# A hand-written order of 887 steps is replaced by another one (attention and a squared-ReLU layer on one core)

## The chip, the cores and the metric

The kernel runs on one core of one Trainium2 chip. The metric is the device time of one execution in microseconds (us), the median of several runs. A core has TensorE (PE; its weight loads are shown apart as PEld), VectorE (DVE), ScalarE (ACT), GpSimd (POOL) and SyncE (SP). Each works through its own instructions in the order in which the program issues them, and waits at an instruction until what it needs is there. SP, POOL and here and there ACT also issue DMAs.

## The reference

Attention over a sliding window of 128 keys plus 4 sink keys, and then a layer with a squared ReLU:

```python
batch, n_heads, seq, head_dim = (4, 8, 768, 64)
scores = scale * np.matmul(q, k.transpose(0, 1, 3, 2))
keep = is_sink | in_window            # 4 sinks, or 0 <= row - column < 128
a = softmax(np.where(keep, scores, -1e9))
x = np.matmul(a, v)  -> (3072, 512)   # heads side by side
h = x @ w_in                          # 512 -> 2048
g = np.maximum(h, 0.0) ** 2
out = g @ w_out                       # 2048 -> 512, float32
```

## The kernel before, in words

The kernel first builds a list of 887 **steps** (class `Op`), each one a small function that issues the instructions of one piece of work, and then issues them in the order of the string `ORDER`. A word of it is a step's number; a letter behind it picks the engine (d VectorE, a ScalarE, g POOL) where a step can run on several, and `+0` or `+1` the pool of PSUM banks where there is a choice. Nothing else sets the order. `Plan.run` goes through the words:

```python
for word in words:
    word, *chosen = word.split("+")
    n = int(word.rstrip("pdag"))
    o = self.ops[n]
    ...
    for s in o.takes:
        if len(s.pools) > 1:
            s.pool = s.pools[int(chosen.pop(0))]
        s.room = free[s.pool].pop(0)
    self.idle = DUMMIES.get(n, 0)
    o.run(o.engine)
    for s in o.reads:
        s.readers -= 1
        if not s.readers:
            free[s.pool].append(s.room)
```

A step that takes a room (a PSUM bank or an SBUF buffer) gets the one that came free first in the order of the list, and its first instruction waits for that room's last readers. There are two pools of two banks in PSUM (`att` and `den`), and rings such as `expm` (8), `r` (3), `osb` (2) in SBUF.

The work is staged by batch (0 to 3), and a batch by three pairs of 128-row tiles (s = 0, 1, 2). In each batch:

- **Loads and turns.** POOL issues loads of q, k and v, 128 KB each, that also convert to bf16 (`load_cast`, `load_v`, `load_natural`, lines L367, L376, L396, L408). In batches 0 and 1 TensorE transposes q and k (L500) and an `unload` copies them out of PSUM; in batches 2 and 3 SP issues transposing DMAs instead (`turn`, L454).
- **Attention.** `scores` (L607; 64-row matmuls, two heads side by side), `sink_scores` (L566) with `sink_keys` (L542) that lays out the sink keys, `expo` (ScalarE, L628), `domask` (VectorE, L637 or L640, or two selects on POOL, L215), `values` (L676), `norm` (VectorE: a reciprocal L692 and a product L693). The result goes back to columns by `bridge` on TensorE (L725) and `bridge_copy`, or, in batches 2 and 3, by a transposing DMA (`turn_x`, L707).
- **Layer 1.** In batches 0 and 1 plain products (L757), a `relu` (L768 on ScalarE, L770 on VectorE) and a `square` (L777, L779). In batches 2 and 3 a Strassen scheme of seven products on blocks half as large (`quad`): sums `xs` of x blocks (L845), once `spread` that separates even and odd rows, sums `wi` of weight blocks (L803, L811), products numbered 1, 2, 5, 4, 3, 6, 7 (L887), a copy `first` of product 1 (t), subtractions from t (L928), a `relu` of the first two quarters (L943), a square (L909 on ScalarE, L911 on VectorE) and a `final` sum with relu (L955).
- **Layer 2.** Plain (L976) for two pairs of batch 0, otherwise again seven products (`layer2_fast`, L1086) with sums of g blocks on VectorE (L1044), copies out of PSUM (L189 on ScalarE and L191 on VectorE, a helper's lines), pair sums (L1111, L1127, L1134) and a store (L1163; L999 in the plain form).

The steps that the prediction speaks of by number: batch 3, pairs 0 and 1: scores 654 and 638 with exps 655, 657 and 639, 641, values 636, sink scores 629. Batch 2, layer 1, pair 0, second quad: products 513 (5), 515 (4), 516 (3), 519 and 520 (6 and 7), relu 517; first quad: products 533 and 534 (6 and 7), final 535, squares 536 and 532, and 518 for the second quad. Batch 2, layer 1, pairs 1 and 2: sum 537, products 569, 570, 573, 575 (1, 2, 5, 4) with copy 571, and 583, 584, 587 (1, 2, 5) with copy 585. Around 105 us: weight sums 361 to 364, layer-2 product 451 and its copy 453, copy 456, sum 468, sink_keys 628 of batch 3, pair sum 457, product 459 (batch 1, pair 0); mask 426. Turn 615 (keys of batch 3, tile 0), turn_x 413, norm 405. Also bridge 123, scores 212 and 663, product 833 with final 827, norms 421 and 428 with scores 431, spread 504; SP's turn 383 and stores 299, 288, 318; POOL's masks 232, 234, 260 and loads 370 to 382 (batch 2) and 610 (batch 3); scores 415.

Of the kernel before, what the change touches and what calls it, by code (L numbers as in the profile page):

```python
# [25 lines left out]
170a 159 160d 177 128 131 165 173d 161d 132d 178d 166d 164a 130a 129a 133a 144 146 136 138 174 145 137 289 290 148  # L26
134 175a 140 135 176a 147d 167d 139d 291 179d 292 293 141d 142 143 149g 42 43 44 45 46 150 151 47 48 49 50 51 52 53
54 365 366 367 368 208g 369 370 371 372 373 294 295 152 154 296 153d 155d 297d 298d 186 187d 180 181a 200+0 204+1
192+0 201 193 205 194a 206d 195a 189 207d 182d 203a 196+0 197 183 198a 190a 191a 188d 199d 202d 274 212+0+0 184d 209
278 279 215 213 237+0+0 210+1 211 238 240 185d 300 301 275 214 302 241d 276 277 303 280 281 282 304 219+0+0 283 222  # L30
220 306a 305 307 230+0+0 309a 233 231 308 311 223 216 221 310 239d 224+0 312 234g 232g 299 385 386 384 383 313 225
314 242+0 217+0 243 218 284 315 316 235+0 236 285 251+0 286a 287a 317d 252d 253d 244+0 246 226+1 228 247d 227d 245a
248+1 229a 399 322 249d 250d 402 400 323d 355 401 256+0+0 259 257 340 254+0 255 341a 258d 358 356 342a 396 260d 334
335a 374 375 376 377 378 379 380 381 395g 388 390 387 288 392 391 318 389 393 394 331 263+0+0 332a 261+1 264 266 319
262 267d 324d 406 333a 407 320a 337 409 265g 382 597 268+0 598 599 600 601 602 603 604 605 606 607 608 609 610 338a
321d 403 269 328 627d 410 270+0 272 404 408 329a 271a 273d 359 325 405 339a 336a 326a 346 347d 357 327a 415 418 419d
330d 352 411 353a 416 412 354d 447 448 343 344a 345a 349 422 423 425 417g 426g 611 451 452 397 363 449 453d 350d 398
450 351a 348a 454 455 457 466 456a 438 458 459 441 439 467 485 486 489 490 487 460 488 461 361 492 431 491a 432 434
615 413 616 622 620 619 493 462 494d 468 463 464a 414 465 621 617 618 420 440g 612 424g 427 496 433g 442g 428 498
421 470 471 443 435g 436 472a 504a 495 362 499 497 500 473 444 437 508 505 469 628 501 475d 474 477 647 429 625 445  # L40
430 446 650 502a 648 624 503 623 626 360 476 478 481 507 479 506 480 364 482 483d 523+0 525a 524 631 527 526 528 634
632 509+0 510 529 511d 512 530 531a 654 538 633 539 513 514 515 655 533 534 657 649g 656g 516 517a 638 613 614 535
635 536d 537 641 519 520 532a 636 658g 651g 521 639 569+0 570 637 571a 629 583+0 630 572 573 585a 640 522a 518a 574
584 587 575 576 586 555+1 642 589 577a 588 643 679 557a 540 556 590 559 591a 592a 578a 558 560 579 580 593 594 581
561 562 595 541+0 542 683 563a 564a 543d 545 544 680 546 565 547 566 548 684 686 644 567 685a 596a 549a 582a 681
550d 689 682 645 484 646 670 551 552 687 690 673 671 674g 553 688a 554a 663 691 694 666 664 665g 568d 698 692 693
699 659 652 702 703 705 667g 672g 695 696d 700 653 717 660 718 721 668 697 661 736a 704a 669 737 675 676 701 722 739
740 738 708 677 678 662 755+1 706 709 741+1 742 757a 719 720 756 743a 723a 707d 759 745 724 758 761 725 744 760 762
763a 764a 711 746 727 710 713 726a 765 766 747 712 769 714 771 767 728 730 715d 772 748 749a 729 815+0 816 817a 732
770 731 818 733 819 751 752 787+1 734a 735 716 801+0 802 803a 789a 753 820 804 768d 821 788 822 773+1 805 791 754a  # L50
823a 824a 775a 790 806 750d 792 829 807 774 793 776 825 808 794 826 809a 827 830 831 795a 796a 810a 777 779 811 778
812 797 798 833 780 834 836 813 799 828a 835a 781a 832 838d 839 783 784 782a 800a 814a 837 840 841 844 785 786d 842
848 849 852 853 855 843 845 846d 867 854a 850 851 858 857d 868 871 847 856 859 873a 861 862 860 863 864 869 872 865a
866 870 877 874 876a 875 878 880 881 886 879 882 883 885 884
"""
DUMMIES = {
    57: 26, 63: 18, 64: 3, 83: 3, 91: 3, 97: 5, 101: 3, 119: 2,
# [1227 lines left out]
```

## Time and profile before

| | |
|---|---|
| median of 3 runs | 213.01 us (212.85 to 213.62) |
| span of the profiled execution, first to last instruction | 210.2 us (210.17) |
| instructions | 5719 |
| TensorE busy | 201.4 us, 96% of the span |
| VectorE, ScalarE, POOL busy | 170.8, 126.6, 101.8 us |
| granted TensorE clock, mean | 0.997 |
| DMA | 26.09 MB, of it 12.59 MB in POOL's converting loads |

The profiled execution's own time is known as its span; the runs' times also hold what lies around it, 2.8 us at the median. Times in microseconds that stand alone (as in "at 131.6") count from the start of the span.

How to read it: the page gives each engine's busy time and, in 40 slices of the span, its busy share in tenths. The chain follows the last instruction back, at each step to what released it. The waits view lists who waited for whom: total, times and the longest. The timeline has one row for neighbouring instructions of a kind: start, duration, engine, line, what it writes from what, and in brackets the idle time before it with what ended it. An engine that is idle but not on the chain costs nothing.

### The profile page before, as it was taken

The page shows a single profiled execution, that of the slowest core. Times are in us where ns is not written, and L with a number is a line of the kernel's source. Part 1 is how long each engine was busy: PE and PEld are TensorE (multiplying, and loading weights), DVE is VectorE, ACT ScalarE, POOL GpSimd, SP SyncE. Part 2 cuts the span into 40 slices and gives each one's busy share as a digit, 9 for nine tenths or more (in the row PEclk, how much of TensorE's full clock was granted, in tenths as well). Part 3 has the DMA queues.
Part 4 walks back from the last instruction along what each step waited for, and adds up shares of the span by engine and source line. Part 5 has one row for each costly group of instructions (what it writes and reads, how often), then busy time and mean ns, then how long its engine had stood idle before and what let it go on. Part 6 is the DMA issues. An engine that isn't in the chain of part 4 may idle for free.

```text
span 210.2 us, 5719 instructions
## 1 busy us (share of the span) xinstructions
PE 201.4 (96%) x2383; PEld 169.4 (81%) x2383; DVE 170.8 (81%) x317; ACT 126.6 (60%) x162; POOL 101.8 (48%) x143
## 2 busy tenths in 40 slices
PE   3999999999999999999999999799999999999993
PEld 3859996689468845679789988699899999999892
DVE  7487567366999964789997988999989978999863
ACT  2498287407744579898952268889870244896110
POOL 7999774898877941999369023700253000000000
PEclk9999999999999999999999999999999999999998
DMA  5999999999999999999987639700512300400222
GB/s 171 278 188 206 171 201 214 161 155 205 153 112 157 104 150 252 138 124 144 149 102 151 103 77 179 50 3 0 150 62 69 75 5 38 166 0 0 103 100 100
DMA packets 93881, 26.09 MB, mean 124 GB/s; under 512 B 86816, under 2 KB 91552, under 8 KB 93856
## 3 DMA queue, kind: packets, MB, share of 16 engines
q0 software_dynamic: 69248, 12.59, 81.3%
q1 hardware_dynamic: 24424, 13.07, 27.9%
q8 instruction: 18, 0.29, 0.6%
q10 hardware_dynamic: 184, 0.07, 0.1%
q14 instruction: 7, 0.06, 0.1%
HBM read 27.30 MB, written 6.29 MB: 160 GB/s over the span
## 4 chain that ended last, share of the span: by engine, by line
PE 94%; DVE 2%; ACT 1%; POOL 1%; issue 1%; POOLq 0%; DVEq 0%
PE py L1086 29%; PE pm L757 20%; PE pm L887 17%; PE po L676 7%; PE py L976 7%; PE ps L607 6%; PE pt L500 3%; PE pt L182 2%; PE px L725 1%; ACT expm L628 1%; PE ya L1086 1%; PE ps L600 1%; PE pk L566 1%; DVE r L955 1%; DVE gT_sb L911 0%
## 5 line engine op out<-in xcount | busy, mean ns | idle before, releaser
L215 POOL TENSOR_SCALAR_AFFINE_SELECT expm<-expm 128x512 bf16<-128x512 bf16 x42 | 29.2, 724 | 49.5 <-ACT expm L628 24.5
L628 ACT ACTIVATE expm<-ps 128x1024 bf16<-128x1024 f32 (+1 forms) x48 | 43.8, 950 | 12.4 <-PE ps L607 11.3
L757 PE MATMUL pm<-xT,w_in_sb 128*128 128x256 bf16 (+1 forms) x320 | 44.7, 294 | 0.0
L757 PEld LDWEIGHTS <-w_in_sb 128*128 128x128 bf16 x320 | 34.2, 114 | 6.6 <-issue 0.9
L1086 PEld LDWEIGHTS <-gT_sb 128*128 128x128 bf16 x336 | 31.1, 98 | 4.2 <-issue 0.5
L1086 PEld LDWEIGHTS <-sg 128*128 128x128 bf16 x240 | 22.8, 98 | 3.3 <-issue 0.5
L768 ACT ACTIVATE r<-pm 128x1024 bf16<-128x1024 f32 x14 | 14.3, 1022 | 13.5 <-PE pm L757 13.4
L887 PEld LDWEIGHTS <-w_in_sb 128*128 128x128 bf16 x256 | 21.8, 114 | 0.5 <-issue 0.2
L887 PE MATMUL pm<-xs,wi 128*128 128x128 bf16 (+1 forms) x192 | 19.5, 246 | 1.5 <-DVE xs L845 0.9
L1086 PE MATMUL py<-wt,gT_sb 128*128 128x256 bf16 x160 | 20.8, 273 | 0.0
L1086 PE MATMUL py<-wt,sg 128*128 128x256 bf16 x160 | 20.6, 273 | 0.0
L909 ACT ACTIVATE gT_sb<-r 128x1024 bf16<-128x1024 bf16 x18 | 18.4, 1051 | 0.3
L1086 PE MATMUL py<-w_out_sb,gT_sb 128*128 128x256 bf16 x144 | 18.5, 273 | 0.0
L189 ACT ACTIVATE osb<-py 128x256 f32<-128x256 f32 (+1 forms) x15 | 6.2, 410 | 20.3 <-DMA out_dram<-osb 6.0
L770 DVE TENSOR_SCALAR r<-pm 128x1024 bf16<-128x1024 f32 x10 | 12.2, 1222 | 7.5 <-PE pm L757 4.3
L887 PEld LDWEIGHTS <-wi 128*128 128x128 bf16 x192 | 16.4, 113 | 2.2 <-issue 2.1
L693 DVE TENSOR_TENSOR xn_sb<-po,rc 128x512 bf16<-128x512 f32 (+1 forms) x28 | 17.2, 615 | 1.0
L676 PEld LDWEIGHTS <-expm 128*128 128x128 bf16 x352 | 16.3, 97 | 1.4 <-issue 0.5
L676 PE MATMUL po<-v,expm 128*128 128x65 bf16 x352 | 17.3, 193 | 0.1
L943 ACT ACTIVATE r<-pm 128x1024 bf16<-128x1024 f32 x12 | 12.1, 1021 | 8.1 <-PE pm L887 7.9
L928 DVE TENSOR_TENSOR t<-t,pm 128x512 f32<-128x512 f32 x24 | 15.9, 680 | 0.9 <-ACT t L189 0.4
L955 DVE CUSTOM_DVE_ANT_1 r<-pm,t 128x1024 bf16<-128x1024 f32 x12 | 14.5, 1220 | 1.6 <-PE pm L887 1.5
(97 smaller groups left out, 381.9 us busy)
## 6 DMA issues: line engine op xcount, KB each, us to landing
out_dram<-osb SPq DMA_DIRECT2D x11, 512.0 KB, 4.5
v<-in_v_dram POOLq DMA_DIRECT2D x24, 128.0 KB, 7.1
qn<-in_k_dram POOLq DMA_DIRECT2D x20, 128.0 KB, 7.1
qn<-in_q_dram POOLq DMA_DIRECT2D x20, 128.0 KB, 6.9
w_in_sb<-in_moe_w_in_dram POOLq DMA_DIRECT2D x4, 512.0 KB, 10.2
w_out_sb<-in_moe_w_out_dram POOLq DMA_DIRECT2D x4, 512.0 KB, 10.4
qr<-in_k_dram SPq DMA_DIRECT2D x4, 256.0 KB, 5.1
qr<-in_q_dram SPq DMA_DIRECT2D x4, 256.0 KB, 4.8
```

The costliest lines, as they stand in the source:

```text
L215: nc.gpsimd.affine_select(out=e_tile, in_=e_tile, compare_op=ALU.is_ge, fill=fill, base=i - 1, pattern=[[0, n], [1 if i else -1, 128]], ch ...
L628: nc.scalar.activation(out=x[:, :, o:512], in_=bank_t["s", b, s, m][:, :, o:512], func=AF.Exp, scale=scale)
L676: touch(("po", b, s, m0), e, nc.tensor.matmul(pv[:, i, h2, :], lhsT=lhsT, rhs=rhs, start=(n_ == 0), stop=(n_ == len(mms) - 1)), j)
L693: touch(("po", b, s, m0), e, nc.vector.tensor_tensor(out=xn_sb[:, 2 * s:2 * s + 2, 128 * (m0 + j0):128 * (m0 + j0 + nj)].rearrange("p i (j ...
L757: nc.tensor.matmul(pm[:, i, :], lhsT=w_in_sb[:, fb // 4, kb, fb % 4:512:4], rhs=xT[:, c0 // 256:(c0 + cw) // 256, kb, :], start=(kb == 0), ...
L768: nc.scalar.activation(out=o, in_=h, func=AF.Relu)
L887: touch(tag, e, nc.tensor.matmul(y[:, bk, i, :], lhsT=weights(name, f0 + i, a), rhs=rhs[:, a, :], start=fresh and i == 0 and a == 0, stop= ...
L909: nc.scalar.activation(out=d, in_=x, func=AF.Square)
L928: touch(tag, e, nc.vector.tensor_tensor(out=T["t"], in0=T["t"], in1=T["y"][:, bk], op=ALU.subtract), bk)
L955: touch(tag, e, nc.vector._custom_dve(TENSOR_ADD_SAT, out=r.rearrange("p b n c -> p b (n c)"), in0=T["y"].rearrange("p b n c -> p b (n c)" ...
L976: touch((b, u), e, nc.tensor.matmul(pm[:, i, :], lhsT=gT_sb[:, fb, 128 * t:128 * t + 128], rhs=w_out_sb[:, fb, :], start=(fb == 0), stop=( ...
L1086: ins = nc.tensor.matmul(y_, lhsT=x[:, i, :], rhs=r_, start=(first or tail and n == 2) and i == 0, stop=i == HB - 1, skip_group_check=not ...
```

## The change

Only the string `ORDER` is replaced. The same 887 steps are issued, with the same matmuls and the same DMAs. The first 25 of TensorE's 290 steps and its last 5 keep their places; between them most steps move by one to twelve places. SP's 60 steps and POOL's (102, now 100) are reordered as well.

61 steps change the engine: 6 relus from VectorE to ScalarE and 4 the other way; 6 squares of plain layer 1 each way; 5 squares of the quads from VectorE to ScalarE and 1 back; 6 copies from ScalarE to VectorE and 2 back in layer 2, with 5 `first_quarter` copies and 1 `evac` from VectorE to ScalarE; 3 unloads and 4 bridge copies from ScalarE to VectorE, 3 bridge copies back; the spread 504 from ScalarE to VectorE; 5 masks from POOL to VectorE and 2 back; sink_values 627 from VectorE to POOL. Three PSUM choices change: 210 and 226 from pool 1 to 0, 244 from 0 to 1.

The places of the two strings that the prediction works on (whole lines of the diff):

```diff
...
-95+0 4 96 117 97 106g 99+1 98 104+0 107 100d 101 118g 81+1 102d 113+0 108d 156 115 127 27 28 29 30 31 32 33 34 35 36
-37 38 116d 82 109+0 111 39 40 41 119+1 121 157a 158a 110 112 120 122 162 123+1 125 163d 168 169d 126a 124a 171 172a
+95+0 4 96 117 97 106g 99+1 98 104+0 107 100d 101 118g 81+1 102d 113+0 108d 156 115 127 116d 82 109+0 119+1 121 120 122
+27 28 29 30 31 32 33 34 35 36 110 157a 111 112 158a 37 38 39 40 41 42 43 44 45 46 47 48 49 50 51 52 53 54 365 162
...
-54 365 366 367 368 208g 369 370 371 372 373 294 295 152 154 296 153d 155d 297d 298d 186 187d 180 181a 200+0 204+1
-220 306a 305 307 230+0+0 309a 233 231 308 311 223 216 221 310 239d 224+0 312 234g 232g 299 385 386 384 383 313 225
-335a 374 375 376 377 378 379 380 381 395g 388 390 387 288 392 391 318 389 393 394 331 263+0+0 332a 261+1 264 266 319
+191d 237+0+0 240 241d 238 300 301 302 239d 281 282 283 219+0+0 304 305 222 220 230+0+0 231 307 233 309a 395g 366 367
+368 369 208g 232g 234g 370 371 372 373 374 375 376 377 378 379 380 381 382 383 221 303 306d 310 223 308 311 224+0 313
+225 210+0 312 211 242+0 314 396 243 284 217+0 218 315 316 299 384 386 385 235+0 236 285 251+0 252d 253d 286a 317a 287a
+357 401 356 258d 340 254+0 332a 255 341a 333d 324d 260g 334 335a 390 389 388 393 387 394 391 392 288 318 263+0+0 264
...
-450 351a 348a 454 455 457 466 456a 438 458 459 441 439 467 485 486 489 490 487 460 488 461 361 492 431 491a 432 434
-615 413 616 622 620 619 493 462 494d 468 463 464a 414 465 621 617 618 420 440g 612 424g 427 496 433g 442g 428 498
+467 447 449 353a 354a 350a 422 346 423 351a 347a 425 343 344a 348a 345a 450 424d 448 363 364 451 453d 452 454 455 438
+361 362 456d 468 607 608 609 610 426g 439 440g 611 413 615 441 442g 612 613 628 457 485 486 458 459 397 462 398 489
...
-632 509+0 510 529 511d 512 530 531a 654 538 633 539 513 514 515 655 533 534 657 649g 656g 516 517a 638 613 614 535
-635 536d 537 641 519 520 532a 636 658g 651g 521 639 569+0 570 637 571a 629 583+0 630 572 573 585a 640 522a 518a 574
+529 530 510 513 635 512 514 633 537 654 531a 533 534 535 536d 538 539 515 516 655 657 614 649g 651g 656g 638 517a 641
+518a 569+0 519 520 636 571a 570 573 642 521 639 572 637 574 640 532a 583+0 584 629 585a 575 587 576 630 522a 586 588
...
```

A word's place in the string sets its place on its own engine's queue; between engines the waits decide.

More of the change, by code (lines that the diff above doesn't have):

```diff
@@ L23 @@
 68d 69+1 85 70 71d 103+0 84+0 105 73g 74d 72d 23 75+1 86 76 77d 91+0 78a 24 87+1 93 25 89 88 92+0 80 26 114+1 90 94
-95+0 4 96 117 97 106g 99+1 98 104+0 107 100d 101 118g 81+1 102d 113+0 108d 156 115 127 27 28 29 30 31 32 33 34 35 36
-37 38 116d 82 109+0 111 39 40 41 119+1 121 157a 158a 110 112 120 122 162 123+1 125 163d 168 169d 126a 124a 171 172a
-170a 159 160d 177 128 131 165 173d 161d 132d 178d 166d 164a 130a 129a 133a 144 146 136 138 174 145 137 289 290 148
-134 175a 140 135 176a 147d 167d 139d 291 179d 292 293 141d 142 143 149g 42 43 44 45 46 150 151 47 48 49 50 51 52 53
@@ L28 @@
-54 365 366 367 368 208g 369 370 371 372 373 294 295 152 154 296 153d 155d 297d 298d 186 187d 180 181a 200+0 204+1
-192+0 201 193 205 194a 206d 195a 189 207d 182d 203a 196+0 197 183 198a 190a 191a 188d 199d 202d 274 212+0+0 184d 209
-278 279 215 213 237+0+0 210+1 211 238 240 185d 300 301 275 214 302 241d 276 277 303 280 281 282 304 219+0+0 283 222
-220 306a 305 307 230+0+0 309a 233 231 308 311 223 216 221 310 239d 224+0 312 234g 232g 299 385 386 384 383 313 225
-314 242+0 217+0 243 218 284 315 316 235+0 236 285 251+0 286a 287a 317d 252d 253d 244+0 246 226+1 228 247d 227d 245a
@@ L33 @@
-248+1 229a 399 322 249d 250d 402 400 323d 355 401 256+0+0 259 257 340 254+0 255 341a 258d 358 356 342a 396 260d 334
-335a 374 375 376 377 378 379 380 381 395g 388 390 387 288 392 391 318 389 393 394 331 263+0+0 332a 261+1 264 266 319
-262 267d 324d 406 333a 407 320a 337 409 265g 382 597 268+0 598 599 600 601 602 603 604 605 606 607 608 609 610 338a
-321d 403 269 328 627d 410 270+0 272 404 408 329a 271a 273d 359 325 405 339a 336a 326a 346 347d 357 327a 415 418 419d
-330d 352 411 353a 416 412 354d 447 448 343 344a 345a 349 422 423 425 417g 426g 611 451 452 397 363 449 453d 350d 398
@@ L38 @@
-450 351a 348a 454 455 457 466 456a 438 458 459 441 439 467 485 486 489 490 487 460 488 461 361 492 431 491a 432 434
-615 413 616 622 620 619 493 462 494d 468 463 464a 414 465 621 617 618 420 440g 612 424g 427 496 433g 442g 428 498
-421 470 471 443 435g 436 472a 504a 495 362 499 497 500 473 444 437 508 505 469 628 501 475d 474 477 647 429 625 445
-430 446 650 502a 648 624 503 623 626 360 476 478 481 507 479 506 480 364 482 483d 523+0 525a 524 631 527 526 528 634
-632 509+0 510 529 511d 512 530 531a 654 538 633 539 513 514 515 655 533 534 657 649g 656g 516 517a 638 613 614 535
@@ L43 @@
-635 536d 537 641 519 520 532a 636 658g 651g 521 639 569+0 570 637 571a 629 583+0 630 572 573 585a 640 522a 518a 574
[L44 to L52, printed above, removed]
@@ L53 @@
-848 849 852 853 855 843 845 846d 867 854a 850 851 858 857d 868 871 847 856 859 873a 861 862 860 863 864 869 872 865a
-866 870 877 874 876a 875 878 880 881 886 879 882 883 885 884
+95+0 4 96 117 97 106g 99+1 98 104+0 107 100d 101 118g 81+1 102d 113+0 108d 156 115 127 116d 82 109+0 119+1 121 120 122
+27 28 29 30 31 32 33 34 35 36 110 157a 111 112 158a 37 38 39 40 41 42 43 44 45 46 47 48 49 50 51 52 53 54 365 162
+123+1 125 168 163d 164a 169a 124d 126d 171 172d 173a 170a 159 160d 165 161d 166d 167d 177 128 131 130a 178a 179a 174
@@ new lines @@
+129d 132d 133d 175d 145 148 149d 176d 137 140 289 290 144 146 141d 147d 136 291 134 135 138 292 150 139d 151 293 142
+143 294 295 152 154 296 274 155d 153a 275 297d 298a 186 187d 183 196+0 276 277 184a 180 185a 181a 278 200+0 201 279
+204+1 205 198a 203a 188d 202d 192+0 182d 206d 194d 193 197 207d 199d 280 195a 212+0+0 213 215 189 216 209 214 190a
+191d 237+0+0 240 241d 238 300 301 302 239d 281 282 283 219+0+0 304 305 222 220 230+0+0 231 307 233 309a 395g 366 367
+368 369 208g 232g 234g 370 371 372 373 374 375 376 377 378 379 380 381 382 383 221 303 306d 310 223 308 311 224+0 313
@@ new lines @@
+225 210+0 312 211 242+0 314 396 243 284 217+0 218 315 316 299 384 386 385 235+0 236 285 251+0 252d 253d 286a 317a 287a
+226+0 244+1 228 246 229d 227a 248+1 247d 245a 399 322 400 402 250d 355 358 249d 256+0+0 331 323a 259 257 360 403 359
+357 401 356 258d 340 254+0 332a 255 341a 333d 324d 260g 334 335a 390 389 388 393 387 394 391 392 288 318 263+0+0 264
+266 265g 267g 261+1 319 406 342d 262 336a 409 407 337 320d 268+0 328 270+0 408 269 410 338a 321a 271d 272 411 273a 412
+329a 330a 339d 325 326d 327d 415 418 419d 416 352 597 598 599 600 601 602 603 627g 604 605 606 404 349 417d 405 466
@@ new lines @@
+467 447 449 353a 354a 350a 422 346 423 351a 347a 425 343 344a 348a 345a 450 424d 448 363 364 451 453d 452 454 455 438
+361 362 456d 468 607 608 609 610 426g 439 440g 611 413 615 441 442g 612 613 628 457 485 486 458 459 397 462 398 489
+420 490 427 492 491a 460 461 487 463 464a 414 504d 421 428 618 619 621 620 465 616 622 493 494a 488 506 469 508 505
+495 507 431 432 434 433d 470 471 496 443 497 473 498 499 444 472d 476 429 617 435g 500 501 436 437 502a 474 523+0 647
+445 430 623 446 626 625 624 503 475d 477 478 481 479 480 482 525a 650 648 524 527 631 526 528 483a 634 632 509+0 511d
@@ new lines @@
+529 530 510 513 635 512 514 633 537 654 531a 533 534 535 536d 538 539 515 516 655 657 614 649g 651g 656g 638 517a 641
+518a 569+0 519 520 636 571a 570 573 642 521 639 572 637 574 640 532a 583+0 584 629 585a 575 587 576 630 522a 586 588
+555+1 643 589 556 577a 557a 590 559 540 679 558 560 591a 578a 592a 579 580 581 593 594 561 562 541+0 542 595 683 582a
+563a 564a 543d 544 545 546 680 681 565 547 566 548 684 686 549a 685a 596a 550a 551 552 567 644 689 688d 682 553 687
+670 690 568a 554a 692 693 698 717 691 694 699 702 671 673 695 700 672d 645 484 646 674g 658g 663 704d 696a 666 703 705
@@ new lines @@
+652 701 719 653 708 664 697 707a 736a 721 706 659 709 675 737 738 660 739 718 676 711 665g 667g 668 669 740 712 710
+713 755+1 741+1 743a 723a 742 756 745 722 714 720 744 746 747 724 661 757a 758 759 748 715a 749a 761 726a 677 662 678
+725 728 727 760 762 750a 763a 764a 729 732 730 771 770 769 765 815+0 766 772 731 733 817a 734a 751 752 816 819 767 735
+716 768a 801+0 787+1 802 818 820 821 822 788 789a 803a 753 754a 804 790 829 773+1 774 805 775a 776 806 807 791 793 777
+808 823a 824a 779 792 831 794 809a 825 826 811 795a 796a 830 778 832 780 812 827 797 833 781a 783 798 784 834 836 810d
@@ L55 @@
+813 782a 828a 835d 799 814a 785 800a 786a 837 840 838d 839 841 844 848 849 842 867 869 843 850 845 852 854a 853 855
+856 851 868 857d 858 870 846a 847 871 872 859 861 873a 862 860 863 864 877 865a 866 874 875 878 876a 880 881 886 879
+883 885 882 884
 """
```

## The prediction

> **What bounds the kernel now.** I read the page's busy shares first, then the slices, then the chain.
>
> ```profile
> PE 201.4 (96%) x2383; PEld 169.4 (81%) x2383; DVE 170.8 (81%) x317; ACT 126.6 (60%) x162; POOL 101.8 (48%) x143
> ...
> PE   3999999999999999999999999799999999999993
> ...
> PE 94%; DVE 2%; ACT 1%; POOL 1%; issue 1%; POOLq 0%; DVEq 0%
> ```
>
> TensorE works in every slice but the first, one in the middle and the last, and 94% of the chain is its own. So this order can be paid only in TensorE's idle time. The waits view, for TensorE alone, lists all of it behind the head:
>
> ```profile
> PE pt L182 <- POOL ident L239: 3.5, 1, 3.5
> PE pm L887 <- DVE xs L845: 0.9, 1, 0.9
> PE pm L887 <- ACT r L943: 0.7, 1, 0.7
> ```
>
> The 3.5 us are the start; the tail from the last matmul (206.7) to the end (210.2) is another 3.5 us. The first 25 TensorE steps and the last 5 are the same in both orders, and so are VectorE's last 5 and SyncE's last 6, so head and tail stay. What can go is 0.68 + 0.86 = 1.54 us, both in the timeline at 130 to 134:
>
> ```profile
> 128.54 1.93 ACT L628 ACTIVATE expm<-ps 128x1024 bf16<-128x1024 f32 x2
> ...
> 130.53 1.02 ACT L943 ACTIVATE r<-pm 128x1024 bf16<-128x1024 f32 x1
> 131.60 1.05 PE L887 MATMUL pm<-xs,wi 128*128 128x128 bf16 x16 [0.68 <-ACT r L943]
> 131.94 1.12 DVE L911 TENSOR_TENSOR gT_sb<-r 128x1024 bf16<-128x1024 bf16 x1
> 132.57 2.92 POOL L215 TENSOR_SCALAR_AFFINE_SELECT expm<-expm 128x512 bf16<-128x512 bf16 x4
> 132.98 0.85 DVE L845 TENSOR_TENSOR xs<-xT 128x512 bf16<-128x512 bf16 x1
> 133.88 0.60 PE L887 MATMUL pm<-xs,wi 128*128 128x256 bf16 x4 [0.86 <-DVE xs L845]
> ```
>
> Products 6 and 7 (519) waited for the relu 517, queued behind two exps; product 1 of the next quad (569) waited for the sum 537, queued behind a final, a mask and a square on VectorE. That stage is full elsewhere too: the windows view has VectorE at 4.82 of 5 us from 130 to 135, and at 4.97 in the next 5.
>
> **Work that stays.** All 2383 matmuls remain, and TensorE's pace per step repeats to 0.01 us in the chain: 0.87 for a layer-2 product (8 matmuls), 0.44 or 0.45 for a layer-1 product, 0.55 for scores. One thing depends on order: a step behind scores costs 0.11 us more.
>
> ```profile
> 59.71 0.44 PE ps L607 x8
> 60.15 0.97 PE py L976 x4
> ...
> 67.59 0.86 PE py L976 x4
> ```
>
> The old order goes 30 times from scores or sink scores to another kind of step, the new one 31 times: **+0.11**. Without any wait the new order is thus 213.01 - 1.54 + 0.11 = 211.6.
>
> **The exchanged engines.** Six relus go from VectorE to ScalarE (1.22 to 1.02, rows L770, L768), four back; six layer-1 squares each way (0.69 against 1.06, L779, L777), five quad squares to ScalarE and one back (L911, L909); three masks net leave POOL (1.23 for two selects) for VectorE (0.69); one sink_values goes to POOL (four of 0.28 become four of 0.49); the rest are copies of 0.4 to 0.6. By these rows VectorE loses some 2.6 us of 171 in all and ScalarE gains 3.8 of 127; neither is full over the whole span, so what decides is where each step lies. One form is not in the trace: the spread 504 on VectorE (128x1024 bf16). Its bounds are 0.69 (L779, the same size) and 1.22 (L770); twice the 512-wide copy (0.42) makes 0.84, and I take that. Behind it on VectorE is norm 421, which the scores 431 need at 112.5; even 1.22 leaves 0.6 us, so it is priced at nothing either way.
>
> **New waits.** I laid the steps' paces end to end in the new order and compared, place by place, with the sum of the rows of what each step needs (0.04 to 0.05 us from one engine to the next, 0.07 overlap between neighbours on one engine, both read off the timeline; a step's first matmul starts 0.17 before its forerunner's modelled end). Most places have something to spare. These do not:
>
> - Scores 638. Between the earlier scores 654 and 638 TensorE now has four products instead of five: 0.56 + 3 x 0.45 = 1.91, less 0.17. ScalarE needs 0.04 + 1.93 (two exps, the row above) + 0.05 to free their banks. **+0.27**, and this hides the 0.68: the relu 517 then ends before 519 starts.
> - Product 573 needs the copy 571. From the end of 516, ScalarE has the relu 1.02, exp 641 0.81, square 518 1.05 and copy 0.60, less overlaps: 3.23. TensorE has 638 0.44, the wait 0.27, 569 0.56, 519 and 520 0.89, values 636 0.36, 570 0.45, less 0.17: 2.80. **+0.48**. The old 0.86 goes, since 537 now stands before the final on VectorE, and 569 needs only that final's end, which comes in time.
> - Product 587 needs copy 585: exp 0.81, square 1.05 and copy 0.60 behind 571 against 573, 583, 584, 629, 575. **+0.13**.
> - Layer-2 product 459 needs the pair sum 457. When layer 1 of batch 1 ends (100.65 on this scale) VectorE has four weight sums of 0.68 (L811), three PSUM reads of 0.41, a sum of 0.70, sink_keys 628 of 0.37 and 457 itself: 4.5 with overlaps, so 105.2, and 459 is due at 105.5. But POOL's mask 426 falls beside them. L811 has rows of 0.68 and one of 1.11. I take 0.45 lost in all: **+0.2**; bounds 0 (no collision) and 0.6 (two rows of 1.11).
> - Small ones: bridge 123 now needs the last of four norms instead of the second (+0.07); scores 212 the last of four unloads (+0.05); scores 663 two exps behind four squares on ScalarE (+0.13); product 833 the final 827 (+0.09); four more of 0.02 to 0.04 (+0.1). **+0.44**; bounds 0 and 0.9, as rows vary by 0.05 in a chain of ten.
>
> Sum: 0.27 + 0.48 + 0.13 + 0.2 + 0.44 = 1.52. The span becomes 210.2 - 1.54 + 0.11 + 1.52 = 210.3. The runs' median lies 2.8 us above the profiled span (213.01 against 210.2), which the order does not touch: **213.1**.
>
> On 459 the trace and the Trainium skill differ in size. In the lines above a sum with two SBUF inputs takes 0.85 instead of 0.42 beside a POOL select. The Trainium skill ("SBUF — State Buffer", Who interferes with whom) says that such an instruction and a GpSimd one that reads SBUF lock each other out for the whole instruction. By that rule both weight sums wait out a whole select (0.72 by the L215 row), 459 waits some 1.1 instead of 0.2, and the total would be 214.0; the row shows 0.43, not 0.72, and I stay with the row.
>
> **The queues that steps are moved past.** SP: the turn 383 now precedes store 299, and the stores 288 and 318 follow all of batch 2's turns: issued near 85.6 instead of 73.7 and 80.4. Store 288 took 8.2 us to land before; even so it lands at 94, and its room is needed at 102. POOL: masks 232 and 234 now precede loads 370 to 382, and mask 260 follows them: 66.2, where 234 ends, + 13 x 0.89 (rows L396, L408: 0.91 and 0.92, issued 0.88 apart) + 1.23 = 79.0, needed at 82.0. The loads feed turns that scores 415 need at 91.8; by rows the last of these lands at 86 to 89.
>
> **Rivals.**
>
> *A, the forecast*: waits of this size appear, the old ones go. 213.1, own range 212.3 to 213.9.
>
> *B, slower: VectorE stands at sink_keys 628 for a DMA.* In the old order 628 ran at 119.3 and its turn 615 was issued at 89.8. In the new one 615 follows turn_x 413 on SP, which waits for norm 405 (96.1): issued at 97.5, and 628 is reached at 104.9 with 457 behind it, for which 459 waits. For it: 413, issued at 97.6 in the old order while loads were queued, is the longest in the view of line L707, 8.1 us:
>
> ```profile
> DMA to landing us min/median/max: 2.4/2.5/8.1
> ```
>
> Against it: the other turns take 2.5 to 7.0 (L454, median 5.3), so 615 would land at 100 to 104.5. It decides from a landing after 104.9. If turns land only behind all loads, then behind load 610 (issued near 100.4, and 3.6 to 6.9 by its rows): 104 to 107.3, or up to 2.4 us of wait. I price it at 1.5: 214.6. The Trainium skill ("DMA: Bandwidth & Descriptors", Queues, rings and completion order) says that each DMA engine takes turns between queues packet by packet. By that rule 615 would be served beside the loads and B would cost nothing; the 8.1 us speak against so simple a reading.
>
> *C, faster: the order closes the gaps.* If ScalarE and VectorE gain a few tenths over my rows at 130 to 137, only some 0.3 us are left: 211.6 to 211.9. Against it: 573's wait is four known rows in a queue.
>
> *D, slower: POOL.* Mask 260 comes over 2.9 us later than worked out, as loads 370 to 382 wait for room in their queue (POOL did so for up to 0.9 us at a time near 25 us). 214 to 215.
>
> **Numbers.** A 0.57, B 0.21, C 0.14, D 0.08. 0.5% (1.07 us, about what a measurement of this kernel can tell from no change) is left downwards by C and a sliver of A: 0.15; upwards by most of B, by D and a sliver of A: 0.28; between them 0.57. The range takes in C and most of B: 211.7 to 215.0. A alone is 212.3 to 213.9.
>
> **What would show it.** Right: TensorE's waits list names L887 behind ACT t (0.5) and scores behind exps (0.3), no xs wait, and all waits behind the head sum to 1.2 to 1.9. B: a DVE row L542 with 1 us or more of idle time near 105, ended by a DMA, and a TensorE wait at L1086 behind it. C: waits below 0.5 in all. D: values 261 late, behind POOL's expm. Wrong: any single TensorE wait over 1 us that is not B's, or steps whose pace differs from the old chain's.

## The result, and the profile after

| | before | after |
|---|---|---|
| median | 212.93 us (212.51 to 213.62, 4 runs) | **215.53 us** (215.19 to 215.88, 4 runs) |
| ratio | | **1.0117, interval 1.0091 to 1.0144** |
| span of the profiled execution | 210.2 us | 213.9 us |
| last matmul's end | 206.7 us | 210.35 us |

The new order is 2.6 us slower, where 0.1 was forecast; 215.5 lies outside the range. Three lines of the page after (TensorE's share of the span, its slices, the chain's shares):

```profile
PE 202.9 (95%) x2383; PEld 168.9 (79%) x2383; DVE 171.5 (80%) x313; ACT 130.3 (61%) x165; POOL 102.7 (48%) x141
...
PE   3989999999999999999999999999997999999993
...
PE 73%; DVE 14%; ACT 5%; DMA 3%; issue 2%; SPq 2%; ACTq 0%; DVEq 0%
```

TensorE's thin slice has moved from 133 us to 163 us, and the chain now runs a good quarter of its way through other engines. The waits view of TensorE (who waited for whom; total, times, longest) names the place; the wait at the start is left out here, and four smaller ones behind:

```profile
...
PE po L676 <- DVE xn_sb L693: 1.6, 2, 1.0
PE pt L500 <- DVE qs L191: 0.6, 2, 0.4
PE py L1086 <- DVE osb L1111: 0.5, 1, 0.5
PE pm L887 <- ACT t L189: 0.3, 1, 0.3
...
```

The old waits for xs (0.9) and for ScalarE's r (0.7) are gone from the list, as forecast. The first line is new: values steps that wait for a norm. To see every step, I laid the paces of the prediction over the new trace and took as a step's delay how much later it ended than its forerunner's end plus its own pace. This finds 1.12 us at values 659 and 0.79 at values 668 (the waits view counts a little less), and smaller delays elsewhere, which the point-by-point section lists. Behind the head, delays sum to 4.6 us; in the old order's trace they sum to 1.9 (0.71 at 519, 1.02 at 569, 0.12 at 576). The difference of 2.7 and the 0.11 for one more exit from scores make 2.8; the medians of the runs differ by 2.6.

The stage around 659, VectorE alone (start, duration, engine, line, output from inputs, and in brackets the idle time before with what ended it):

```profile
156.81 1.11 DVE L1044 TENSOR_TENSOR sg<-sg,gT_sb 128x1024 bf16<-128x1024 bf16 x1
157.85 1.12 DVE L640 TENSOR_TENSOR expm<-expm,tri 128x1024 bf16<-128x1024 bf16 x1
158.88 0.41 DVE L191 COPY osb<-py 128x256 f32<-128x256 f32 x1
159.22 0.78 DVE L1044 TENSOR_TENSOR sg<-gT_sb,sg 128x1024 bf16<-128x1024 bf16 x1
159.92 1.12 DVE L1044 TENSOR_TENSOR sg<-sg,gT_sb 128x1024 bf16<-128x1024 bf16 x1
160.96 0.20 DVE L692 RECIPROCAL rc<-po 128x8 f32<-128x8 f32 x1
161.19 0.69 DVE L693 TENSOR_TENSOR xn_sb<-po,rc 128x512 bf16<-128x512 f32 x1
161.80 0.41 DVE L1111 TENSOR_TENSOR osb<-py,osb 128x256 f32<-128x256 f32 x1
163.67 0.49 DVE L845 TENSOR_TENSOR xs<-xd 128x256 bf16<-128x256 bf16 x2 [1.45 <-ACT xd L189]
```

Values 652 end at 159.32, so norm 653 (L692 and L693) could start then. It starts at 160.96, because the sums 701 and 719 stand ahead of it, and before them sum 700 and mask 672 have taken 1.11 and 1.12 instead of 0.68. TensorE's values 659 need the room that 653 reads, and 659 begins 1.1 us late. Then VectorE stands 1.45 us at xs 737, with norm 660 behind it, for which values 668 wait. ScalarE in the same stage:

```profile
162.31 0.38 ACT L189 ACTIVATE u<-py 128x256 f32<-128x256 f32 x1 [3.16 <-DVE osb L1111]
162.59 1.05 ACT L189 ACTIVATE xd<-xT 128x1024 bf16<-128x1024 bf16 x1
```

The spread 736 (xd) could run when ScalarE's exps are done (159.15), but stands behind copy 707, and 707 waits for VectorE's pair sum 708, though it doesn't use its result: ScalarE is idle for 3.16 us. Both read the same bank of one PSUM tile (regions "a" and "d" of L1065). `use` calls `touch` (L196 to L203), which frees two readers on different engines from each other only where they read different banks and both are marked `alone`. So here whichever stands first in the list must end first. And POOL:

```profile
156.09 6.63 POOL L215 TENSOR_SCALAR_AFFINE_SELECT expm<-expm 128x512 bf16<-128x512 bf16 x8 [22.62 <-ACT expm L628]
```

Four masks in one row, right beside VectorE's slow steps. Mask 658 could have run at 133 (its exp ended at 132.9), but the new order puts it behind 674, whose exp ends at 156.

The same stage in the old order, with VectorE's rows around norms 653 and 660, the spread on ScalarE, and POOL:

```profile
155.96 0.78 DVE L1044 TENSOR_TENSOR sg<-sg,gT_sb 128x1024 bf16<-128x1024 bf16 x1
156.66 0.20 DVE L692 RECIPROCAL rc<-po 128x8 f32<-128x8 f32 x1
156.89 0.69 DVE L693 TENSOR_TENSOR xn_sb<-po,rc 128x512 bf16<-128x512 f32 x1
157.49 0.87 DVE L1044 TENSOR_TENSOR sg<-gT_sb 128x1024 bf16<-128x1024 bf16 x1
158.28 0.19 DVE L692 RECIPROCAL rc<-po 128x8 f32<-128x8 f32 x1
...
155.10 1.06 ACT L189 ACTIVATE xd<-xT 128x1024 bf16<-128x1024 bf16 x1 [0.29 <-issue]
...
154.88 4.56 POOL L215 TENSOR_SCALAR_AFFINE_SELECT expm<-expm 128x512 bf16<-128x512 bf16 x6 [2.98 <-ACT expm L628]
```

POOL had three masks there too (665, 667, 672), and VectorE's sums were stretched as well, by 0.48 in all. But norm 653 came 0.52 after values 652 had ended (156.14), with one sum between two norms, and the spread ran early.

### The profile page after: what moved, and what is told of

Same layout as the page of the kernel before. It is cut to its first block, busy times and chain, and to the rows that moved or that the text cites. A ratio compares the mean times of both kernels' runs of the same rounds, so it can differ in the third digit from the quotient of the medians.

```text
span 213.9 us, 5706 instructions
## 1 busy us (share of the span) xinstructions
PE 202.9 (95%) x2383; PEld 168.9 (79%) x2383; DVE 171.5 (80%) x313; ACT 130.3 (61%) x165; POOL 102.7 (48%) x141
## 4 chain that ended last, share of the span: by engine, by line
PE 73%; DVE 14%; ACT 5%; DMA 3%; issue 2%; SPq 2%; ACTq 0%; DVEq 0%
PE py L1086 21%; PE pm L887 17%; PE pm L757 16%; PE po L676 6%; PE py L976 5%; PE ps L607 4%; DMA qr<-in_q_dram 3%; DVE sg L1044 3%; ACT expm L628 2%; DVE expm L640 2%; PE pt L500 2%; SPq L346 2%; DVE w_in_sb L811 1%; PE px L725 1%; DVE xn_sb L693 1%
## 5 line engine op out<-in xcount | busy, mean ns | idle before, releaser
L215 POOL TENSOR_SCALAR_AFFINE_SELECT expm<-expm 128x512 bf16<-128x512 bf16 x36 | 26.8, 776 | 46.6 <-ACT expm L628 46.5
L909 ACT ACTIVATE gT_sb<-r 128x1024 bf16<-128x1024 bf16 x22 | 22.4, 1056 | 1.8 <-DVE r L955 1.6
L189 ACT ACTIVATE osb<-py 128x256 f32<-128x256 f32 (+1 forms) x17 | 7.2, 422 | 23.8 <-DVE osb L1134 12.3
L676 PEld LDWEIGHTS <-expm 128*128 128x128 bf16 x352 | 16.8, 97 | 4.3 <-POOL expm L215 1.2
L676 PE MATMUL po<-v,expm 128*128 128x65 bf16 x352 | 18.3, 193 | 1.9 <-DVE xn_sb L693 1.6
L768 ACT ACTIVATE r<-pm 128x1024 bf16<-128x1024 f32 x16 | 16.4, 1023 | 5.2 <-PE pm L757 5.2
L887 PE MATMUL pm<-xs,wi 128*128 128x128 bf16 (+1 forms) x192 | 18.9, 246 | 0.2 <-DVE r L955 0.2
L693 DVE TENSOR_TENSOR xn_sb<-po,rc 128x512 bf16<-128x512 f32 (+1 forms) x28 | 17.2, 615 | 1.0
L928 DVE TENSOR_TENSOR t<-t,pm 128x512 f32<-128x512 f32 x24 | 16.1, 684 | 1.1 <-PE pm L887 0.2
L777 ACT ACTIVATE gT_sb<-r 128x1024 bf16<-128x1024 bf16 x13 | 13.6, 1061 | 4.7 <-DVE r L770 4.5
L976 PE MATMUL py<-w_out_sb,gT_sb 128*128 128x512 bf16 x64 | 15.8, 380 | 0.0
L943 ACT ACTIVATE r<-pm 128x1024 bf16<-128x1024 f32 x12 | 12.2, 1025 | 5.6 <-PE pm L887 4.9
```

The source lines that it names most:

```text
L215: nc.gpsimd.affine_select(out=e_tile, in_=e_tile, compare_op=ALU.is_ge, fill=fill, base=i - 1, pattern=[[0, n], [1 if i else -1, 128]], ch ...
L676: touch(("po", b, s, m0), e, nc.tensor.matmul(pv[:, i, h2, :], lhsT=lhsT, rhs=rhs, start=(n_ == 0), stop=(n_ == len(mms) - 1)), j)
L693: touch(("po", b, s, m0), e, nc.vector.tensor_tensor(out=xn_sb[:, 2 * s:2 * s + 2, 128 * (m0 + j0):128 * (m0 + j0 + nj)].rearrange("p i (j ...
L768: nc.scalar.activation(out=o, in_=h, func=AF.Relu)
L777: nc.scalar.activation(out=g, in_=r, func=AF.Square)
L887: touch(tag, e, nc.tensor.matmul(y[:, bk, i, :], lhsT=weights(name, f0 + i, a), rhs=rhs[:, a, :], start=fresh and i == 0 and a == 0, stop= ...
```

## The experiments

The theories: **T1**, the steps stand in the wrong order in VectorE's and ScalarE's queues, so that steps due later (sums, copies) hold steps due now (norms, the spread). **T2**, contention: POOL's masks slow VectorE's steps with two SBUF inputs, and the stage is late for that. **T3**, what part of the difference is the single execution's head. **T4**, the exchanged engines cost the time. All times below are medians; the old order's runs beside them had medians of 212.66 to 212.86. Diffs are of the words of the order.

**before_again**: no edit.

> The kernel before, unchanged, for a second profile of it. Theory T3 (the head of the new order's profile, 0.84 us longer than in the old one's profile with the same steps, is a matter of the single execution: when the first loads land): the median stays at 213.0 within 0.5, but this profile's span need not be 210.2; with what lies around the span at 1.7, as in the four runs of the new order, it should be near 211.2, and TensorE's step 76 (the last transposes of the first tile, 11.6 in the first profile) may come up to 1 us later. Rival: the head of the old order is always as in its first profile; then step 76 ends at 12.0 to 12.2 again and the span is 210.2 within 0.2.

Measured: 212.98 us (ratio 1.0015, 0.9998 to 1.0033), span 210.7; TensorE's step 76 began at 12.19, against 11.65 in the first profile. The span lies between the two numbers expected (211.2 and 210.2). In the runs whose spans are known 1.7 to 2.1 us lie around the span, mostly 1.7. So the first profiled execution took about 211.9, at the low end of this kernel's runs, and its head was a lucky one: over 14 profiles TensorE's first 25 steps, the same in all, end 0 to 1.5 us later than in it, in part as the first loads land. In the trace after, VectorE waits there 2.7 us in all for `qr<-in_q_dram`, 1.0 in the first trace before. T3 holds for 0.84 us of the 3.7 between the two profiled spans, and for nothing in the medians. From here on, delays are counted behind the head.

**spread_first**

```diff
-652 701 719 653 708 664 697 707a 736a 721 706
+652 701 719 653 708 664 697 736a 707a 721 706
```

> The new order with one pair swapped on ScalarE: the spread 736 ahead of the copy 707. Theory T1 (queues): 707 waits on ScalarE for VectorE's pair sum 708 (3.16 us idle), holds the spread behind it, and so VectorE stands 1.45 us at xs 737, with norm 660 behind it, for which values 668 waits 0.79. Then the spread ends at 160.2, xs 737 has no wait, norm 660 starts with the end of values 659, and TensorE's 0.79 at 668 is 0 to 0.1: 214.7. T2 (contention: what makes the stage late is that VectorE's sums take 1.1 beside POOL's four masks): VectorE is late anyway and 668 keeps over 0.5 of its wait: 215.2 to 215.5.

Measured: 214.53 us (ratio 1.0097, 1.0074 to 1.0120). The 0.79 at 668 is gone, the 1.11 at 659 stays; delays behind the head 3.5 instead of 4.6. T1 for 668, by the trace: between the ratios of this run and the new order 0.4 us lie, which is within their intervals. ScalarE shows both halves of the argument:

```profile
158.47 1.07 ACT L189 ACTIVATE xd<-xT 128x1024 bf16<-128x1024 bf16 x1
161.69 0.38 ACT L189 ACTIVATE u<-py 128x256 f32<-128x256 f32 x1 [2.15 <-DVE osb L1111]
```

The spread runs as soon as ScalarE's exps are done, and copy 707 still waits for pair sum 708, now at nobody's cost.

**both_norms**: the swap above, and

```diff
-652 701 719 653 708 ... 709 675 737 738 660 739
+652 653 701 719 708 ... 709 660 675 737 738 739
```

> The new order with the spread 736 ahead of copy 707 on ScalarE, and on VectorE norm 653 ahead of the sums 701 and 719, and norm 660 ahead of xs 737 and 738. T1 (queues): the sums stay slow (1.1 beside POOL's masks) but are in nobody's way: values 659 loses its 1.12, values 668 keeps 0.1 of its 0.79: 215.5 - 1.8 = 213.7. T2 (contention): the slow sums are late for the products behind them (701 for 709, 719 for 725) and half of the gain is lost there: 214.6.

Measured: 214.19 us (1.0080, 1.0059 to 1.0101). 659 has no delay, as T1 says; 668 keeps 0.29 and product 741 gets 0.24, since sum 719, still 1.11 long, stands ahead of 660. Sums and mask kept their 0.96 to 1.12. So the gain is 0.8 by the ratios (each good to some 0.5), not 1.8, between the two theories' numbers: T2's slow sums do take a part back.

**mask_early**

```diff
-649g 651g 656g 638 517a 641 ... 646 674g 658g 663
+649g 651g 656g 658g 638 517a 641 ... 646 674g 663
```

> The new order with one POOL step moved: mask 658 (its exp is done at 132.9) ahead of mask 674 instead of behind it, so that POOL runs it near 133.5 and not at 157.3. T2 (contention): with POOL idle from 157.4 to 159.2 mask 672 and sum 701 on VectorE take 0.7 instead of 1.12 and 0.78, norm 653 ends some 0.5 to 0.75 sooner, and the waits at 659 and 668 (1.91 together) fall to 0.7 to 1.3; near 134 VectorE's two-input steps get slower instead (537 and 538 from 0.42 to 0.6 or more), which costs 0 to 0.3 there: 214.4 to 215.1. T1 (queues): the rows change little and the waits stay above 1.5: 215.3 to 215.6.

Measured: 215.65 us (1.0151, 1.0125 to 1.0176), no gain, as T1 had said. But the rows go T2's way at both places. From 157.5 to 159.3, with POOL idle, mask 672 takes 0.68 and sum 701 0.67, and the delay at 659 falls to 0.57 (with 668's 0.79 it makes 1.36, where T2 had 0.7 to 1.3). But 658 now runs from 132.8 to 134.4, and there VectorE has:

```profile
132.91 1.04 DVE L911 TENSOR_TENSOR gT_sb<-r 128x1024 bf16<-128x1024 bf16 x1
133.88 1.18 DVE L845 TENSOR_TENSOR xs<-xT 128x512 bf16<-128x512 bf16 x2
```

Square 536 took 0.69 and the two xs 0.76 in the new order. The final 521 behind them ends later, and product 583 waits 0.71, where I had expected 0 to 0.3. The mask took its contention along to a fuller place.

**early_fixed**

```diff
-240 241d 238 300 301 302
+240 300 241d 238 301 302
...
-221 303 306d 310 223 308
+221 306d 303 223 310 308
...
-455 438 361 362 456d 468 ... 613 628 457 485 486
+455 438 456d 457 468 ... 613 485 486
...
+433d 361 362 470 ... 475d 628 477
```

> The new order with VectorE's steps moved at three places before 110 us, each ahead of or behind a step that nobody waits for: sum 300 ahead of mask 241; copy 306 ahead of sum 303 and mask 223 ahead of pair sum 310; pair sum 457 right behind copy 456, the weight sums 361 and 362 behind mask 433, sink_keys 628 behind 475. On a scale on which the old order takes 212.7 the new one takes 215.2. T1 (queues: each wait of TensorE is a step standing behind a step that is due later): the waits at 304 (0.26), 308 (0.13), 224 (0.40) and 459 (0.64) go, 1.4 in all: 213.8. Rival (VectorE is full, so a wait taken away here comes back at the next product that needs VectorE): at most 0.5 is kept: 214.7 or more, with new waits between 110 and 125.

Measured: 214.31 us (1.0069, 1.0045 to 1.0093), 1.0 less than the new order by the ratios. The delays at 304, 308, 224 and 459 are all gone, with no new one between 60 and 130 us, so T1 by the trace; the time lies between the two theories' numbers.

**late_fixed**

```diff
-652 701 719 653 708 664 697 707a 736a 721 706 659 709 675 737 738 660 739 718 676 711 665g
+652 653 701 708 664 697 736a 707a 721 706 659 709 660 675 737 738 739 676 718 711 719 665g
...
-715a 749a 761 726a
+715a 726a 749a 761
```

> The new order changed only behind 155 us: on ScalarE spread 736 ahead of copy 707 and copy 726 ahead of relu 749; on VectorE norm 653 ahead of sum 701, norm 660 ahead of xs 737, norm 669 and the sums 718 and 719 placed by their due times. Same scale (old 212.7, new 215.2). T1 (queues): the waits at 659 (1.12), 668 (0.79) and 762 (0.41) go, 2.3 in all, though VectorE's sums still take 1.1 beside POOL's masks: 212.9. T2 (contention): the stage keeps more than half of it, because the slow sums only move the wait: 214.1 or more.

Measured: 213.75 us (1.0050, 1.0030 to 1.0070), 1.4 less. The delays at 659, 668 and 762 are gone, so T1 by the trace, though the time lies between the theories' numbers: norm 669 stood behind sum 718, copy 711 and sum 719, and product 741 waited 0.67 for it: my own move, by the same mechanism.

**all_fixed**: both sets, with `633` behind `535` and `642` behind `521`.

> Both sets of moves together, and on VectorE masks 633 and 642 behind the finals 535 and 521. T1 (queues): the gains add up (1.4 + 2.3 + 0.2 at product 569): 211.3, which is 0.6% below the old order; what is left of TensorE's waits is 0.43 at 573 and some tenths. Rival (gains are lost to each other as VectorE has no room): 212.5 to 213.5, no better than the old order.

Measured: 212.78 us (0.9998, 0.9985 to 1.0012), 2.5 less than the new order: the two gains add (1.0 and 1.4), as T1 said, but the time falls into the rival's range. 1.5 us are missing against the 211.3 expected, and the trace shows most of it as delays that the moves made: 0.67 at 741, 0.30 at 305, 0.22 at 683, 0.17 at 576.

**engines_only**: the old string with the new string's letters.

> The old order of steps with the new order's engines (61 steps change the engine, none changes its place). T1 (the loss comes from the order of the queues): within 0.6 of the old order, 212.1 to 213.3. Rival T4 (the loss comes from the exchanged engines: ScalarE's new squares, VectorE's new copies and masks): 214 or more.

Measured: 240.65 us (1.1312, 1.1269 to 1.1356), neither theory's number. TensorE is delayed at over 20 places, by up to 3.3 us (values 268). This says that places and engines are one choice. It doesn't say what the exchanges cost within the new order. What the other runs say on T4: all_fixed and the kernel best below keep every engine of the new order, and its loss goes all the same, so the exchanges alone don't cost it. But three steps of the stage around 659 are exchanged ones: mask 672 came to VectorE from POOL (1.12 us ahead of norm 653), copy 704 from ScalarE (0.41), and copy 707 went from VectorE to ScalarE, where it holds the spread. No run puts these back, and so the exchanges' share in that stage stays open.

**best**: all_fixed, with `301` too ahead of `241d`, `642` back ahead of `521`, and

```diff
-676 718 711 719 665g 667g 668 669 740
+676 665g 667g 668 669 718 711 719 740
```

> The new order with both sets of moves, cleaned of what they cost: sum 301 as well ahead of mask 241 (product 305 had a new wait of 0.30), norm 669 ahead of 718, 711 and 719 (product 741 had a new wait of 0.67), mask 642 left ahead of final 521 (576 and 683 had 0.17 and 0.22), mask 633 behind final 535. T1 (queues; the gains of separate stages add): 212.8 - 0.67 - 0.30 - 0.39 = 211.4, ratio to the old order 0.994. Rival (such waits come back elsewhere as VectorE is full): 212.3 or more, ratio 0.998 or above.

Measured: 212.51 us (0.9982, 0.9968 to 0.9996). The delays behind the head are 1.5 against the old order's 1.9, and the ratio is just below 1: a gain over the old order of 0.2%, a third of what T1 expected, and the rival's number (0.998). The waits view of TensorE, without the wait at the start and a small one behind:

```profile
...
PE pt L500 <- DVE qs L191: 0.5, 1, 0.5
PE pm L887 <- ACT t L189: 0.3, 1, 0.3
PE pm L887 <- DVE t L928: 0.3, 1, 0.3
...
```

The first is the head; the second is product 573; the third is product 747, 0.42 by the paces, which became the next one due.

**best_b**

```diff
-641 518a 569+0 519 520 636 571a 570
+641 569+0 519 636 520 571a 518a 570
```

> As the kernel best, and values 636 ahead of product 520 on TensorE and copy 571 ahead of square 518 on ScalarE. The forecast gave product 573 a wait of 0.48 (0.43 seen) because copy 571 stands behind square 518. T1 (it is that queue): with 571 right behind the end of values 636, whose room it takes, 573's wait goes, and 0.2 to 0.27 comes at 636 (its exp 641 ends at 134.7 where 636 is then due at 134.5): 0.2 below the kernel best. Rival (the wait belongs to the chain from scores 638 over exp 641 and values 636, and no order of 518 and 571 changes it): no gain, or a small loss.

Measured: 212.59 us (0.9992, 0.9980 to 1.0005): no gain. 573's wait is gone and 636 waits 0.25, as T1 said, but product 583 now waits 0.60 for final 521 (0.18 before), since product 520, which 521 needs, runs after 636. The local argument was right and the next step in line took the gain.

**old_537**

```diff
-614 535 635 536d 537
+614 537 535 635 536d
```

> The old order with one step moved: xs 537 ahead of final 535 on VectorE, where VectorE stands idle for 0.50 us. T1 (a step in the idle place costs nothing and its wait goes): product 569 loses its 0.86, sink scores 629 gets 0.1 to 0.25 of wait for exp 639: 212.7 - 0.7 = 212.0, ratio 0.997. Rival (what is late next is as late: final 521 for product 583, copy 571 for 573): within 0.2 of the old order.

Measured: 212.54 us (0.9989, 0.9974 to 1.0004): within what can be told from the old order. The delay at 569 is gone, and 0.18 at 629 (exp 639), 0.37 at 583 (final 521) and 0.31 at 576 stand in its place, where the old order has 0, 0 and 0.12: the rival.

**no_masks**: `if n not in (658, 674, 665, 667)` ahead of a step's `run`.

> The new order without the four masks that POOL runs between 156 and 163 (658, 674, 665, 667; they are left out, so the output lacks them), all else as it was. T2 (contention: VectorE's sums are slow only because POOL's masks run beside them): sums 700, 701, 719 and mask 672 fall from 1.11, 0.78, 1.12 and 1.12 to 0.68 each, norm 653 ends 1.4 sooner, 659 loses its 1.12 and 668 most of its 0.79, though 653 and 660 keep their late places in the order: 1.5 to 1.9 less than the new order, 213.3 to 213.7 on the scale where the old one takes 212.7. T1 (the places in the queues alone): the sums stay above 0.9 without masks and the waits stay: 215. If both are needed, order and contention, this run and the one with the moved norms must each remove most of the 1.9.

Measured: 213.94 us (1.0046, 1.0031 to 1.0061), 1.5 less than the new order. VectorE with POOL idle (the line numbers are one higher):

```profile
157.09 0.68 DVE L1045 TENSOR_TENSOR sg<-sg,gT_sb 128x1024 bf16<-128x1024 bf16 x1
157.69 0.68 DVE L641 TENSOR_TENSOR expm<-expm,tri 128x1024 bf16<-128x1024 bf16 x1
158.29 0.41 DVE L192 COPY osb<-py 128x256 f32<-128x256 f32 x1
158.62 0.68 DVE L1045 TENSOR_TENSOR sg<-gT_sb,sg 128x1024 bf16<-128x1024 bf16 x1
159.22 0.68 DVE L1045 TENSOR_TENSOR sg<-sg,gT_sb 128x1024 bf16<-128x1024 bf16 x1
```

Every stretched step is back at 0.68. Norm 653 starts 0.23 after values 652 end instead of 1.64, and 659's 1.12 is gone, though 653 keeps its late place; 668 keeps 0.44, for the spread. So 659's wait needs both things, and taking away either the masks (here) or the place (both_norms) removes it. For 668 the place of the spread is enough, and contention adds to it.

## Why the prediction was wrong, point by point

**What failed** is the sentence ahead of the list of new waits, "Most places have something to spare. These do not", and with it that list (1.52). It held none of the three delays behind 150 us: 659 (1.12), 668 (0.79), 762 (0.41), in all 2.32, where 2.4 lie between 213.1 and 215.5. That the two agree so well is partly luck: the other delays came to 2.25 instead of 1.52, the old waits had cost 1.85 by the paces and not 1.54, and the traces differ by 0.2 more than the medians. Two things had been left out of the sums for those places.

- **Contention.** I had read 0.43 more for a VectorE sum beside a POOL select off the old trace, and used it at one place only (459). The new order runs eight selects in a row beside sums 700, 701, 719 and mask 672: 0.43 + 0.10 + 0.44 + 0.44 = 1.4 us on VectorE, all ahead of norm 653. With the rows of a step alone, as the sums had them, 659 would not have been late: so it is in no_masks.
- **A wait that isn't in the data.** Copy 707 behind pair sum 708, and pair sum 727 behind copy 726, which itself stood behind a relu:

```profile
174.49 0.42 DVE L1111 TENSOR_TENSOR osb<-py,osb 128x256 f32<-128x256 f32 x1 [2.81 <-ACT u L189]
174.83 0.68 DVE L928 TENSOR_TENSOR t<-t,pm 128x512 f32<-128x512 f32 x1
```

VectorE idles 2.81 us at 727, and the subtraction 760 (L928) behind it is what product 762 waits for. ScalarE's relu 749 had to wait for product 748 until 173.16, and copy 726 came after it. The Trainium skill ("PSUM — Partial Sum Buffer", PSUM bank collisions raise a hardware error) says that the compiler's scheduler adds a dependency between any two instructions on different engines that touch the same bank and quadrant, reads alike. The 3.16, 2.15 and 2.81 us agree with an order kept between such readers; in this kernel `touch` leaves it in wherever the bank is the same.

The prediction's paragraph on the exchanged engines said that where each step lies decides. That was right, but it priced them over the whole span: by its rows VectorE was to lose 2.6 us, and its busy time rose by 0.7 (170.8 to 171.5). Mask 672 and copy 707, two of the exchanged steps, stand in the stage that was late.

**The steps that held.** Head and tail kept their steps (the tail is 3.5 again), and the paces fit. The old waits went: 519 keeps 0.06. The spread 504 took 0.81 (taken as 0.84). **573**: 0.48 forecast (3.23 less 2.80 and 0.05 between engines), 0.43 seen, in this order's every profile.

**The terms that were mis-sized.** The old waits left more behind than thought: 569 is still delayed by 0.21, for final 535, of which the forecast said "which comes in time". **638**: 0.27 forecast, none seen. Exp 655 begins 0.10 before the modelled end of scores 654, not 0.04 after it (130.95 against 131.05): it needs only the first six of the twelve matmuls, which end at 130.88. So the two exps end when TensorE is there. **587**: 0.13 forecast, none seen, as 573 and what follows are late together. **459**: 0.2 with bounds 0 and 0.6; seen 0.64, and 0.53 to 0.55 in five other profiles. The last three rows of VectorE ahead of 459 (none has idle time before it):

```profile
106.14 0.68 DVE L1044 TENSOR_TENSOR sg<-sg,gT_sb 128x1024 bf16<-128x1024 bf16 x1
106.74 0.34 DVE L542 COPY kblk<-qkT 64x16 bf16<-64x16 bf16 x2
107.11 0.42 DVE L1111 TENSOR_TENSOR osb<-py,osb 128x256 f32<-128x256 f32 x1
```

One of the four weight sums took 1.11 and one 0.78, near what was allowed for (0.45); what I missed is that VectorE began them 0.43 after layer 1 had ended (102.52 against 102.09), with mask 424 and sum 448 ahead of them. **Small ones**: 0.44 forecast, but the places were wrong: 123, 212 and 663 show nothing, 833 shows 0.05, while 224 has 0.40 (mask 223 behind pair sum 310), 304 has 0.26 (sum 300 behind mask 241), 308 has 0.13 and 422 has 0.07.

**The rivals.** B didn't happen: the L542 row above has no idle time, so turn 615 had landed. D didn't happen: mask 260 ran from 78.8 to 81.3, 2.3 later than worked out and not the 2.9 that D needed, and values 261 began at 83.4. C didn't happen. The slower result came by a mechanism that no rival had.

**The 2.8 us around the span** were 1.7, and 1.1 by which the profiled execution was faster than the median; its head accounts for 0.6 of that against the median of the 14 profiles. The sum stayed right, since it ended at the median.

On the rule of the Trainium skill ("SBUF — State Buffer", Who interferes with whom), by which the two instructions lock each other out, the trace agrees, and setting it against the row of 0.43 was a misreading. Three of POOL's eight selects in the stage around 659, to be laid beside VectorE's rows there:

```profile
157.34 1.08 POOL L215 TENSOR_SCALAR_AFFINE_SELECT expm<-expm 128x512 bf16<-128x512 bf16 x1
158.38 1.08 POOL L215 TENSOR_SCALAR_AFFINE_SELECT expm<-expm 128x512 bf16<-128x512 bf16 x1
159.41 1.08 POOL L215 TENSOR_SCALAR_AFFINE_SELECT expm<-expm 128x512 bf16<-128x512 bf16 x1
```

The selects end at 158.42, 159.46 and 160.50, mask 672 and the sums 701 and 719 at 158.96, 160.00 and 161.04: each 0.54 after the select ahead of it. And each of these selects ends 0.50 after the VectorE step ahead of it (sum 700 ends at 157.92). So the two engines take turns, one instruction each, and a row holds the wait for the turn as well. Alone, a sum takes 0.68 and a select 0.61. What a sum loses is the rest of the select that has the turn: 0.43 or 0.44 where the sum was next in VectorE's queue, 0.10 for sum 701, which came when the select had 0.24 to go, and nothing where POOL has to wait instead (weight sum 356 at 79.1 took its 0.68, and mask 260's first select beside it 1.49). The prediction's price by the rule (a whole select for each sum) was too high; for 459 two sums lost 0.43 and 0.10. Steps with a PSUM input keep their time (norm's product 0.69 beside masks and without).

## What to carry to other kernels

When a new order is judged, list for every stage what stands ahead of each step in its engine's queue with the durations it has beside its new neighbours, not the alone ones; in this kernel a mask on POOL cost VectorE up to 0.44 us for each sum of two SBUF inputs that it met, and it took that price along when it was moved (mask_early). Count as waits also the order that the framework keeps between two engines' reads of one PSUM bank. And look at what is due next: in early_fixed nothing else was, and all four delays went; in late_fixed product 741 took 0.67 of the 2.3 back; in old_537 and best_b the next step was as late, and no gain can be told.

## What had not been expected of the hardware

- A VectorE sum of two SBUF inputs and a POOL select go strictly one after the other, and either engine's row shows the wait as busy time: 128x1024 sums of 0.68 read as 0.78 to 1.12, selects of 0.61 as 1.08. One last_quarter sum (461; 128x256 f32, 0.42 alone) took 1.48 beside mask 442 in the new order and ended 0.29 after it.
- The first 19 us vary by up to 1.5 us from one execution to the next, with the same instructions, in part by when the first q and k loads land. A single profiled span is no base for a sum of a few tenths; the median is.
